# First products by block sums in tiles 3 to 6, with casts moved to GpSimd

## The chip, the cores and the metric

The kernel runs on one core of a Trainium2 chip. The metric is the device time of one execution in microseconds. The engines are TensorE (PE, with its weight loads shown apart as PEld), VectorE (DVE), ScalarE (ACT), GpSimd (POOL) and SyncE (SP, which only issues transfers here). GpSimd issues transfers too, between its own instructions.

## What is computed

Two stages follow each other: attention in a window of 32 positions, and a feed-forward block with the tanh form of GELU on its output.

```python
def _attn_ref(q, k, v):            # 8 batches, 8 heads, 576 positions, 64 wide
    scores = scale * np.matmul(q, k.transpose(0, 1, 3, 2))
    mask = np.abs(pos[:, None] - pos[None, :]) <= 32
    scores = np.where(mask, scores, -1000000000.0)
    attn = np.exp(scores - np.max(scores, axis=-1, keepdims=True))
    attn = attn / (np.sum(attn, axis=-1, keepdims=True) + 1e-09)
    return np.matmul(attn, v)

def _moe_ref(x, w_in, w_out):      # 4608 tokens, 512 wide, 2048 hidden
    h = x @ w_in
    g = 0.5 * h * (1.0 + np.tanh(c * (h + 0.044715 * h * h * h)))
    return g @ w_out
```

Everything comes and goes in float32; the products run in float16 with float32 sums.

## The kernel before

**Tiles.** The 4608 tokens are cut into nine tiles of 512, numbered t = 0 to 8. A batch holds 576 tokens, so batch b = t + 1 has its attention computed while tile t is in its second product, and its columns go into a ring `xT` of 1536 tokens.

**A tile's first stage** multiplies by `w_in`. The 2048 hidden columns are 16 blocks of 128, numbered n; block n stands at column `n // 2 + 8 * (n % 2)`. One block is four matmuls of 512 columns (`ffn_in`, L577), then one GELU on ScalarE (`gelu`, L585, or L657 in `in_mixed`) into `gT`. The first three matmuls of blocks 0 to 2 run ahead of the stage's last attention columns. After every fourth block `sums` (L694) forms four sums of GELU results on VectorE for the second stage.

**A tile's second stage** multiplies by `w_out` in steps i = 0 to 111, one matmul of 256 columns each (`ffn_out`, L751): seven products of 16 steps. This is the scheme of Strassen in Winograd's form, where four quarter matrices need seven products in place of eight, and sums of quarters are formed beforehand. The table `WINO` lists which sums are multiplied; `new` says that a product starts a bank instead of adding to it. After each product VectorE takes the result into `yo` (L762 to L789), which the next use of the same bank waits for. GpSimd issues the output stores (L713, L711) after product 5 and at the end.

**Attention in the second stage.** The dictionary `PLAN` hangs steps of attention onto the steps i: `s` scores and exponentials, `m` the mask on VectorE, `v` the weighted values and the denominators, `x` the multiplication into `xT` (L540). `@0` and `@1` name one of two pairs of PSUM banks, `S0` and `S1`; without one, `v` uses the banks `O` and `D`. Group -1 is the tail of the batch before.

**Queries and keys.** For b >= 4 these are loaded as float32 by SyncE (`load_qk`), cast to float16 on VectorE at the start of the tile's first stage (`turn_queries` L410, `turn_keys` L419, `turn_tails` L430), and turned by transposing transfers on SyncE's queue (L413, L421, L431). V is loaded and cast by a GpSimd transfer (L216, L220) at steps 4 and 7, after a small copy on GpSimd (`after`, L989) that waits for the key tail's transpose. `pair_v` (L225, L226) makes shifted copies of V on VectorE.

**Order.** Each engine runs its instructions in the order in which the program issues them; nothing rearranges them. A tile buffer that is used again waits for its last readers, and for a store that reads it until that store has landed.

**Tiles 7 and 8** do eight of their 16 blocks by seven products as well, in two groups of four blocks, A and B (`in_mixed`, L629). `in_w` forms four sums of quarters of `w_in` (L604), `in_x` four differences of quarters of `xT` (L614). The list `MIX` is the order of one such stage: a number is a plain block, `A0` or `B0` a product, `s0A` a copy of a bank into SBUF (L644), `cA00` an addition onto that copy (L649), `g` a GELU, and `t` and `u` the first and the last two of the four sums. A product that adds to a bank waits for the copy or the addition that reads it first. `WINO` and `MIX` share the same seven products:

```python
WINO = [("A11", "B11", True), ("S2", "T2", True), ("A12", "B21", False), ("S3", "T3", False),
        ("S1", "T1", True), ("A22", "T4", False), ("S4", "B22", False)]
```

**Buffers.** The pool `rawp` has two buffers each under the names `qr` and `kr`, 8 KB per partition, which take turns for raw queries, keys, V of batches 2 and 3, and in tiles 7 and 8 for `in_w`'s sums of A and the copies. The pool `yp` has two buffers under the name `yo`. They hold in turn two scratch tiles of batch 0, a score tile, the last two output row blocks of tile 0 (`yo` of `ffn_out_0`, kept in `later` and stored in tile 2), and the sums of group B.

Of the kernel before, what the change touches and what calls it, by code (L numbers as in the profile page):

```python
# [36 lines left out]
def cut(b):  # L37
# [5 lines left out]

PLAN = {7: "s0@0 s1@1 v-1", 16: "m0 m1 x-1", 33: "s2@0 v0@1 v1", 36: "m2", 44: "x0", 50: "x1",
        62: "s3@0 s4@1 v2", 66: "m3", 80: "x2", 84: "m4", 91: "v3", 112: "x3"}


# [11 lines left out]

MIX = ("3 g3 A0 s0A B0 s0B 12 g12 A2 B2 cA00 cB00 A1 s1A gA00 A4 B1 s1B gB00 B4 t0 u0 13 g13 A3 s3A B3 s3B 14 g14 "
       "cA11 cB11 A5 gA10 B5 gB10 gA11 gB11 A6 B6 cA01 cB01 15 gA01 gB01 t1 t2 g15 t3 u1 u2 u3").split()
UNITS = {"A": 1, "B": 2}

PLAN_1 = {12: "s0@0 s1@1 s2", 16: "m0 m1", 36: "m2", 56: "s-1@0 v0@1 v1", 62: "m-1 x0", 64: "x1",
# [4 lines left out]
          [(t4, 12 + i + j) for i in (0, 2) for t4 in (0, 3, 1, 2) for j in range(2)]  # L71


RING = 1536
LOW = -30000.0

# [2 lines left out]
def kernel(  # L79
# [26 lines left out]

    const = ctx.enter_context(tc.tile_pool(name="const", bufs=1))
    big = ctx.enter_context(tc.tile_pool(name="big", bufs=1))
    rawp = ctx.enter_context(tc.tile_pool(name="rawp", bufs=2))
    hp = ctx.enter_context(tc.tile_pool(name="hp", bufs=1))  # L110
    tailp = ctx.enter_context(tc.tile_pool(name="tailp", bufs=1))
    pep = ctx.enter_context(tc.tile_pool(name="pep", bufs=3))
# [24 lines left out]
    def load_early(b):  # L137


        qr = rawp.tile([128, H, 256], FP32, name="qr")  # L140
        kr = rawp.tile([128, H, 256], FP32, name="kr")
        raws[b] = [qr, kr, None]

        def qk(h0, queues=(nc.sync, nc.sync)):
            for src, dst, queue in zip((q, k), (qr, kr), queues):
                queue.dma_start(
                    dst[:, h0:h0 + 2, :],
                    src[b, h0:h0 + 2, 0:512, :].rearrange("h (p j) d -> p h (j d)", j=4))

        def vs(*cs):  # L150
            if len(raws[b]) < 4:
                raws[b].append(stage.tile([128, 4, H, 64], FP32, name="vr", tag="stage"))
                raws[b].append(tailp.tile([128, 4, 64], FP32, name="vt", tag="vt"))
            for c in cs:
                if c == 4:
                    for x in range(2):
                        nc.sync.dma_start(raws[b][4][64 * x:64 * x + 64, :, :],
                                          v[b, 4 * x:4 * x + 4, 512:S, :].rearrange("h p d -> p h d"))
                else:
                    nc.sync.dma_start(raws[b][3][:, c, :, :],  # L160
                                      v[b, :, 128 * c:128 * c + 128, :].rearrange("h p d -> p h d"))

        def tails(which="qk"):
            if raws[b][2] is None:
                raws[b][2] = tailp.tile([128, H, 64], FP32, name="tr", tag="tr")
            tr = raws[b][2]
            if b == 0:
                for i, src in enumerate((q, k)):
                    for x in range(2 if "qk"[i] in which else 0):
                        nc.sync.dma_start(tr[64 * x:64 * x + 64, 4 * i:4 * i + 4, :],  # L170
                                          src[b, 4 * x:4 * x + 4, 512:576, :].rearrange("h s d -> s h d"))
                return
            for h in (0, 4):
                for x, src in enumerate((q, k)):
                    nc.sync.dma_start(tr[64 * x:64 * x + 64, h:h + 4, :],
                                      src[b, h:h + 4, 512:576, :].rearrange("h s d -> s h d"))

        return qk, tails, vs

    def load_qk(b):  # L180


        if b == 3:
            qr = raws[3]
        else:
            qr = rawp.tile([128, H, 256], FP32, name="qr")
            load_q(b, qr)
        kr = rawp.tile([128, 4, H, 64], FP32, name="kr")
        if b > 3:
            qt = tailp.tile([16, H, 256], FP32, name="qt", tag="vt")  # L190
            kt = tailp.tile([64, H, 64], FP32, name="kt", tag="tr")
            raws[b] = (qr, kr, qt, kt)
        else:
            raws[b] = [qr, kr, tailp.tile([128, H, 64], FP32, name="tr", tag="tr"), None]
        for c in range(4):
            nc.sync.dma_start(kr[:, c, :, :],
                              k[b, :, 128 * c:128 * c + 128, :].rearrange("h p d -> p h d"))
        load_tails(b, nc.sync)
        if b == 3:
            load_vr(3)  # L200
# [199 lines left out]


    def load_vr(b):
        vr = vrs[b] = rawp.tile([128, 4, H, 64], FP32, name="qr")
        for c in range(4):
            nc.sync.dma_start(vr[:, c, :, :],
                              v[b, :, 128 * c:128 * c + 128, :].rearrange("h p d -> p h d"))

    def turn_queries(b, src, dst, p0, p1):
        for pr in range(NPAIR):
            nc.vector.tensor_copy(  # L410
                dst[:, pr, :, :, :].rearrange("p j h d -> p h j d"),
                src[:, 2 * pr:2 * pr + 2, :].rearrange("p h (j d) -> p h j d", j=4))
        nc.sync.dma_start_transpose(QTs[b].rearrange("d r j p -> d (r j) p")[:, :, p0:p1],  # L413
                                    dst.rearrange("p r j h d -> p (r j h d)"))

    def turn_keys(b):
        k16, kr = halfs[b][1], raws[b][1]
        for pr in range(NPAIR):
            nc.vector.tensor_copy(k16[:, pr, :, :, :], kr[:, :, 2 * pr:2 * pr + 2, :])  # L419
            if pr % 2:  # L420
                nc.sync.dma_start_transpose(  # L421
                    KTs[b % 2][:, pr - 1:pr + 1, :].rearrange("d r (c p) -> d (r c) p", c=4),
                    k16[:, pr - 1:pr + 1, :, :, :].rearrange("p r c h d -> p (r c h d)"))

    def turn_tails(b):
# [1 line left out]
        qt16 = hp.tile([16, NPAIR, 4, 2, 64], FP16, name="qt16", tag="qt16")  # L427
        kt16 = hp.tile([64, NPAIR, 2, 64], FP16, name="kt16", tag="t16")
        turn_queries(b, qt, qt16, 128, 144)
        nc.vector.tensor_copy(kt16.rearrange("p r h d -> p (r h d)"), kt.rearrange("p h d -> p (h d)"))  # L430
        nc.sync.dma_start_transpose(  # L431
            KLs[b % 2], kt16.rearrange("p r h d -> p (r h d)"))

# [157 lines left out]
    def in_w(eng, unit, *which):  # L591
# [1 line left out]
        i, j = UNITS[unit] // 2, 2 * (UNITS[unit] % 2)  # L593
        A11, A12, A21, A22 = (w_cols[:, d:d + 2, c + i, j:j + 2, :] for c in (0, 2) for d in (0, 2))
        if (unit, "s") not in mixed:
            halves = [(rawp if unit == "A" else yp).tile([128, 2, 2, 2, 128], FP16, name="wc" + unit + str(x),
                                                         tag=("qr", "kr")[x] if unit == "A" else "yo") for x in range(2)]
            mixed[unit, "s"] = [half[:, x] for half in halves for x in range(2)]
        S1, S2, S3, S4 = mixed[unit, "s"]
        mixed[unit, "w"] = dict(A11=A11, A12=A12, A22=A22, S1=S1, S2=S2, S3=S3, S4=S4)  # L600
        for x in which:
# [4 lines left out]
    def in_x(t):  # L606

        pos = t * 512 % RING
        B11, B12, B21, B22 = (xT[:, d:d + 2, pos + c:pos + c + 256] for d in (0, 2) for c in (0, 256))
        xc = hp.tile([128, 4, 2, 256], FP16, name="xc", tag="q16" if t % 2 else "k16")  # L610
        T1, T2, T3, T4 = (xc[:, x] for x in range(4))
        mixed["x"] = dict(B11=B11, B21=B21, B22=B22, T1=T1, T2=T2, T3=T3, T4=T4)
        for dst, a, b in ((T1, B12, B11), (T2, B22, T1), (T3, B22, B12), (T4, B21, T2)):
            nc.vector.tensor_tensor(dst, a, b, op=ALU.subtract)  # L614

    def in_product(unit, n):
        a, w, new = WINO[n]
        if n == 0:
            phs[unit, "a"] = psO.tile([128, 512], FP32, name="pu", tag="O") if unit == "A" else bank(1)
        elif n in (2, 4):  # L620
            which = "b" if n == 2 else "c"
            if unit == "A":
                phs[which] = psS.tile([128, 2, 512], FP32, name="pu2", tag="S1" if n == 2 else "S0")
            phs[unit, which] = phs[which][:, "AB".index(unit), :]
        ps = phs[unit, "b" if n == 2 else "c" if n in (4, 6) else "a"]
# [4 lines left out]
                                 start=(n in (0, 2, 4) and h == d == 0), stop=(h == d == 1), skip_group_check=True)  # L630

    def in_mixed(t):
        if "A" not in mixed:
            mixed["A"] = rawp.tile([128, 3, 512], FP32, name="sa", tag="qr")
            mixed["B"] = rawp.tile([128, 3, 512], FP32, name="sb", tag="kr")

        place = {"00": (0, "b"), "01": (1, "c"), "11": (2, "c")}
        for step in MIX:
            kind, rest = step[0], step[1:]
            if kind in UNITS:  # L640
                in_product(kind, int(rest))
            elif kind == "s":
                n, unit = int(rest[0]), rest[1]
                (nc.scalar.copy if n == 1 or rest == "3B" else nc.vector.tensor_copy)(  # L644
# [285 lines left out]
    for t in range(NT):  # L930
        b = t + 1
        att = b < B
        if t:
# [8 lines left out]
            elif att:  # L942
                if b > 3:
                    open_and_turn(b)
                turn_keys(b)
                if b > 3:
                    turn_tails(b)
            if t >= NT - 2:
                if t == NT - 2:
                    in_x(t)  # L950
                in_mixed(t)
            for fc in range(begun, NF if t < NT - 2 else 0):
                ffn_in(t, fc)
                if t == 1 and fc == 3:
                    turn_keys(2)
                    load_vr(2)
                    raws[2] = [None, None, raws[2][2], vrs[2], tailp.tile([64, H, 64], FP32, name="vt", tag="vt")]
                    nc.sync.dma_start(raws[2][4], v[2, :, 512:S, :].rearrange("h p d -> p h d"))
                    raws[3] = rawp.tile([128, H, 256], FP32, name="qr")
                    load_q(3, raws[3])  # L960
                    combine(4, nc.vector)
                if t == 1 and 6 <= fc < 10:
# [24 lines left out]
        for i in range(113 if t else 65):  # L987
# [67 lines left out]
                    spread(*group(g), *ods[g])  # L1055
            if t == NT - 2 and i == 84:
                in_x(t + 1)
            if t in (3, 4) and i == 52:
                in_w(nc.vector, "B", *((1, 2) if t == 3 else (3, 4)))
            if t == NT - 3 and i in (52, 86):  # L1060
                in_w(nc.vector, "A", *((1, 2) if i == 52 else (3, 4)))
            if t == 2 and i in (40, 44):
                store(0, *later[1 if i == 40 else 3])
            if t == 1 and i == 30:
                cast_vt(2)
                store(0, *later[0])
# [43 lines left out]
```

## Time and profile before

| | us |
|---|---|
| three runs | 297.32, 299.41, 296.19 |
| median | 297.32 |
| profiled execution | 296.65 |
| its span, first to last instruction | 294.6 |
| mean granted TensorE clock | 0.997 |
| start of the first stage of tiles 3, 4, 5, 6 and 7 | 115.67, 146.09, 176.57, 206.99, 237.40 |
| length of the first stage of tiles 3 to 6 | 13.8 |
| length of the first stage of tiles 7 and 8 | 13.3 |

A row of a timeline gives the start and the length in microseconds, the engine, the line, the operation, what it writes and reads, the shape, and how many like it were merged; in brackets stands how long the engine was idle before it and what ended that. L577 is line 577 of the listing. PE's matmuls overlap, so one that is shown with 379 ns follows the one before by less. "To landing" is the time from a transfer's issue to its end. A stage's row in the table by stage gives its limits, its length, and for each engine the busy time and the count.

### The profile page before, as it was taken

The numbers are of one execution on the slowest core, as the hardware profiler recorded it, in microseconds if no ns is written. First come the engines' busy times: TensorE is split into PE (matmuls) and PEld (weight loads), VectorE is DVE, ScalarE is ACT, GpSimd is POOL, SyncE is SP. The second block draws the span as 40 slices with busy tenths as digits, with TensorE's granted clock in tenths as the row PEclk, the third lists the DMA queues.
The fourth block names the chain that finished last, engine by engine and source line by source line (L and its number), as shares of the span: only waits on it lengthen the run. The fifth ranks groups of instructions, "written<-read, shape, count | busy, mean of one in ns | idle before, by whom it ended". The sixth has DMA issues, their size and how long they took to land.

```text
span 294.6 us, 7286 instructions
## 1 busy us (share of the span) xinstructions
PE 285.9 (97%) x2945; PEld 192.7 (65%) x2945; DVE 212.4 (72%) x467; ACT 196.5 (67%) x315; POOL 88.8 (30%) x143
## 2 busy tenths in 40 slices
PE   8889999999999999999999999999999999999993
PEld 3535545547765687568755885588558867887783
DVE  4755477998897667858796878686957877865762
ACT  5965877777677874787667776796669558706800
POOL 4445335004228713205250615050800050025000
PEclk9999999999999999999999999999999999999998
DMA  7999998999999998999999999899691040004013
GB/s 229 275 380 396 359 305 196 254 186 203 248 229 202 251 202 188 113 139 245 162 212 94 246 157 191 116 245 154 117 190 7 0 118 28 2 26 120 0 47 99
DMA packets 114392, 51.02 MB, mean 173 GB/s; under 512 B 98471, under 2 KB 110247, under 8 KB 114102
## 3 DMA queue, kind: packets, MB, share of 16 engines
q1 hardware_dynamic: 89460, 38.67, 62.4%
q0 software_dynamic: 23776, 10.83, 23.4%
q10 hardware_dynamic: 1122, 1.06, 1.1%
q8 instruction: 23, 0.38, 0.6%
q14 instruction: 11, 0.09, 0.1%
HBM read 36.70 MB, written 9.44 MB: 157 GB/s over the span
## 4 chain that ended last, share of the span: by engine, by line
PE 85%; DVE 5%; DMA 5%; issue 1%; SPq 1%; ACT 1%; POOL 0%; DVEq 0%
PE mm L751 32%; PE ph L577 17%; PE mm L577 16%; PE ps_s L468 4%; PE pu L629 3%; DMA kr<-in_k_dram 3%; PE mm L723 2%; DMA wst<-in_moe_w_in_dram 2%; PE py L723 2%; PE ps_d L495 2%; PE ps_o L505 2%; DVE t L684 2%; DVE s L694 1%; PE mm L629 1%; PE ps_od L495 1%; PE ps_od L505 1%
## 5 line engine op out<-in xcount | busy, mean ns | idle before, releaser
L577 PEld LDWEIGHTS <-w_in 128*128 128x128 f16 x512 | 57.4, 113 | 49.8 <-POOL w_in L250 1.5
L577 PE MATMUL ph<-xT,w_in 128*128 128x512 f16 x256 | 64.5, 379 | 0.6 <-POOL w_in L250 0.6
L577 PE MATMUL mm<-xT,w_in 128*128 128x512 f16 x256 | 64.1, 379 | 0.0
L585 ACT ACTIVATE gT<-mm 128x512 f16<-128x512 f32 x60 | 35.6, 598 | 33.3 <-PE mm L577 32.7
L713 POOL DMA_DIRECT2D out_dram<-y x55 | 32.8, 605 | 82.4 <-DVE y L780 75.3
L751 PEld LDWEIGHTS <-s 128*128 128x128 f16 x512 | 49.3, 98 | 7.1 <-DVE s L694 0.6
L751 PE MATMUL mm<-t,s 128*128 128x256 f16 x376 | 45.2, 273 | 0.2 <-DVE y L764 0.2
L694 DVE TENSOR_TENSOR s<-gT 128x512 f16<-128x512 f16 x64 | 27.5, 430 | 19.1 <-ACT gT L585 18.9
L751 PEld LDWEIGHTS <-gT 128*128 128x128 f16 x384 | 36.2, 98 | 6.4
L585 ACT ACTIVATE gT<-ph 128x512 f16<-128x512 f32 x58 | 32.4, 604 | 10.9 <-PE ph L577 10.9
L481 ACT ACTIVATE pe<-ps_s 128x960 f16<-128x960 f32 (+1 forms) x31 | 29.5, 975 | 13.2 <-PE ps_s L468 13.1
L751 PE MATMUL mm<-w_out,gT 128*128 128x256 f16 x256 | 32.6, 273 | 0.0
L104 ACT ACT_TABLE_LOAD x18 | 23.1, 1283 | 2.2 <-issue 1.9
L530 ACT ACTIVATE lt<-ps_d 128x480 f32<-128x480 f32 (+2 forms) x28 | 15.6, 556 | 10.4 <-PE ps_d L495 6.9
L531 ACT ACTIVATE lt<-lt 128x480 f32<-128x480 f32 (+3 forms) x36 | 21.1, 585 | 1.1
L490 DVE TENSOR_TENSOR pe<-pe,band 128x960 f16<-128x960 f16 x28 | 18.5, 680 | 2.0 <-ACT pe L481 1.9
L505 PEld LDWEIGHTS <-V 128*64 128x64 f16 x520 | 13.7, 111 | 5.5 <-DVE V L226 1.5
L751 PE MATMUL mm<-t,gT 128*128 128x256 f16 x128 | 16.1, 273 | 0.0
L694 DVE TENSOR_TENSOR s<-s,gT 128x512 f16<-128x512 f16 x32 | 14.0, 436 | 1.1
L216 POOL DMA_DIRECT2D V<-in_v_dram x16 | 14.3, 908 | 1.1 <-PE ps_s L468 0.4
L751 PE MATMUL mm<-w_out,s 128*128 128x256 f16 x120 | 14.6, 273 | 0.0
L540 DVE TENSOR_TENSOR xT<-ps_o,lt 128x480 f16<-128x480 f32 (+5 forms) x26 | 13.4, 535 | 1.6 <-PE ps_o L505 1.6
(149 smaller groups left out, 390.3 us busy)
## 6 DMA issues: line engine op xcount, KB each, us to landing
kr<-in_k_dram SPq DMA_DIRECT2D x31, 256.0 KB, 10.2
qr<-in_q_dram SPq DMA_DIRECT2D x6, 1024.0 KB, 5.9
wst<-in_moe_w_in_dram SPq DMA_DIRECT2D x8, 512.0 KB, 6.6
wst<-in_moe_w_out_dram SPq DMA_DIRECT2D x2, 1024.0 KB, 10.5
wst<-in_moe_w_out_dram SPq DMA_DIRECT2D x4, 512.0 KB, 7.4
qr<-in_v_dram SPq DMA_DIRECT2D x8, 256.0 KB, 6.5
V<-in_v_dram POOLq DMA_DIRECT2D x16, 128.0 KB, 8.5
qr<-in_q_dram SPq DMA_DIRECT2D x7, 256.0 KB, 7.3
```

Source lines behind the costliest of these rows:

```text
L104: nc.scalar.add_instruction(mybir.InstLoadActFuncSet(name=nc.get_next_instruction_name(), act_func_set_id=which, ins=[], outs=[]))
L216: nc.gpsimd.dma_start(V[:, c, :, :], v[b, :, 128 * c:128 * c + 128, :].rearrange("h p d -> p h d"))
L481: nc.scalar.activation(pe, ps[:, :, 0:w], AF.Exp, scale=SCALE)
L490: nc.vector.tensor_tensor(pe, pe, m.rearrange("k (o j) p -> k o j p", o=1).broadcast_to(list(pe.shape)), op=ALU.mult)
L505: nc.tensor.matmul(o[64 * h:64 * h + 64, cols].rearrange("d (j p) -> d j p", j=4)[:, :, p0 - q0:p1 - q0], Vs[b % 2][:, slot, 2 * pr + h, : ...
L530: nc.scalar.activation(lt[:, 0:n], d[:, 0:n], AF.Ln)
L531: nc.scalar.activation(lt[:, 0:n], lt[:, 0:n], AF.Exp, scale=-1.0)
L577: nc.tensor.matmul(ph, w_cols[:, dc, fc // 4, fc % 4, :], xT[:, dc, t * 512 % RING:t * 512 % RING + 512], start=(dc == 0), stop=(dc == 3))
L585: nc.scalar.activation(gTs[t][:, fc, :], phs[fc], AF.Gelu_apprx_tanh)
L694: nc.vector.tensor_tensor(dst, x, y, op=op)
L713: eng.dma_start(out_v[b, j, q0 + p:q0 + p + e, cols], yo[m:m + e, cols])
L751: nc.tensor.matmul(pys["apart"][:, 0:256] if apart else py[:, blk, :], lhsT, wino[w][:, f, :], start=(new and i % (8 if one else 16) == 0) ...
```

## The change

In tiles 3 to 6 the four blocks of group B (n = 8 to 11) are done by seven products, with a list `MIX_1` for the order, group A staying plain. The banks are those of group A in tiles 7 and 8. The key casts, the query-tail casts and the key-tail cast of batches 4 to 7 move from VectorE to GpSimd; the main query casts stay. `rawp` gets one buffer under each of four names, `q0`, `q1`, `k0` and `k1`. The sums of B's weights, formed in tiles 3 and 4 before, are formed in tile 2; the two stores of `yo` in tile 2 stand at steps 8 and 12 of the program instead of 40 and 44. `v1` moves from step 33 to step 36, and `pair_v` stands in `MIX_1`.

```diff
-PLAN = {7: "s0@0 s1@1 v-1", 16: "m0 m1 x-1", 33: "s2@0 v0@1 v1", 36: "m2", 44: "x0", 50: "x1",
+PLAN = {7: "s0@0 s1@1 v-1", 16: "m0 m1 x-1", 33: "s2@0 v0@1", 36: "m2 v1", 44: "x0", 50: "x1",
         62: "s3@0 s4@1 v2", 66: "m3", 80: "x2", 84: "m4", 91: "v3", 112: "x3"}
...
+MIX_1 = ("3 B0 g3 s0B 4 B2 cB00 B1 s1B g4 5 g5 6 g6 t0 u0 B3 s3B gB00 pair B4 7 g7 cB11 gB11 12 g12 t1 u1 B5 gB10 B6 cB01 gB01 13 g13 14 g14 t2 u2 15 g15 t3 u3").split()
...
+LONE = 3
...
-    rawp = ctx.enter_context(tc.tile_pool(name="rawp", bufs=2))
+    rawp = ctx.enter_context(tc.tile_pool(name="rawp", bufs=1))
...
     def turn_queries(b, src, dst, p0, p1):
         for pr in range(NPAIR):
-            nc.vector.tensor_copy(
+            (nc.gpsimd if p0 and b > LONE else nc.vector).tensor_copy(
...
     def turn_keys(b):
-            nc.vector.tensor_copy(k16[:, pr, :, :, :], kr[:, :, 2 * pr:2 * pr + 2, :])
+            (nc.gpsimd if b > LONE else nc.vector).tensor_copy(k16[:, pr, :, :, :], kr[:, :, 2 * pr:2 * pr + 2, :])
...
-        nc.vector.tensor_copy(kt16.rearrange("p r h d -> p (r h d)"), kt.rearrange("p h d -> p (h d)"))
+        (nc.gpsimd if b > LONE else nc.vector).tensor_copy(kt16.rearrange("p r h d -> p (r h d)"), kt.rearrange("p h d -> p (h d)"))
...
-        xc = hp.tile([128, 4, 2, 256], FP16, name="xc", tag="q16" if t % 2 else "k16")
+        xc = rawp.tile([128, 4, 2, 256], FP16, name="xc", tag="k1") if t < NT - 2 else \
+            hp.tile([128, 4, 2, 256], FP16, name="xc", tag="q16" if t % 2 else "k16")
...
-    def in_product(unit, n):
+    def in_product(unit, n, alone):
         a, w, new = WINO[n]
         if n == 0:
-            phs[unit, "a"] = psO.tile([128, 512], FP32, name="pu", tag="O") if unit == "A" else bank(1)
+            phs[unit, "a"] = psO.tile([128, 512], FP32, name="pu", tag="O") if unit == "A" or alone else bank(1)
         elif n in (2, 4):
             which = "b" if n == 2 else "c"
-            if unit == "A":
+            if unit == "A" or alone:
...
-        for step in MIX:
+        for step in MIX if t >= NT - 2 else MIX_1:
             kind, rest = step[0], step[1:]
-            if kind in UNITS:
-                in_product(kind, int(rest))
+            if step == "pair":
+                pair_v(t + 1, nc.vector.tensor_copy)
+            elif kind in UNITS:
+                in_product(kind, int(rest), t < NT - 2)
...
                 if b > 3:
                     open_and_turn(b)
+                if t >= LONE:
+                    in_x(t)
                 turn_keys(b)
                 if b > 3:
                     turn_tails(b)
...
-            for fc in range(begun, NF if t < NT - 2 else 0):
+            elif t >= LONE:
+                in_mixed(t)
+            for fc in range(begun, NF if t < LONE else 0):
...
-            if t in (3, 4) and i == 52:
-                in_w(nc.vector, "B", *((1, 2) if t == 3 else (3, 4)))
+            if t == LONE - 1 and i in (52, 86):
+                in_w(nc.vector, "B", *((1, 2) if i == 52 else (3, 4)))
...
-            if t == 2 and i in (40, 44):
-                store(0, *later[1 if i == 40 else 3])
+            if t == 2 and i in (8, 12):
+                store(0, *later[1 if i == 8 else 3])
```

Left out above are the new tags in the calls that allocate from `rawp`.

More of the change, by code (lines that the diff above doesn't have):

```diff
@@ L137, in load_early @@
     def load_early(b):
-        qr = rawp.tile([128, H, 256], FP32, name="qr")
-        kr = rawp.tile([128, H, 256], FP32, name="kr")
+        qr = rawp.tile([128, H, 256], FP32, name="qr", tag=f"q{b}")
+        kr = rawp.tile([128, H, 256], FP32, name="kr", tag=f"k{b}")
         raws[b] = [qr, kr, None]
@@ L185, in load_qk @@
         else:
-            qr = rawp.tile([128, H, 256], FP32, name="qr")
+            qr = rawp.tile([128, H, 256], FP32, name="qr", tag="q0")
             load_q(b, qr)
-        kr = rawp.tile([128, 4, H, 64], FP32, name="kr")
+        kr = rawp.tile([128, 4, H, 64], FP32, name="kr", tag="k1" if b == 3 else "k0")
         if b > 3:
@@ L402, in load_vr @@
     def load_vr(b):
-        vr = vrs[b] = rawp.tile([128, 4, H, 64], FP32, name="qr")
+        vr = vrs[b] = rawp.tile([128, 4, H, 64], FP32, name="vr", tag="q1")
         for c in range(4):
@@ L595, in in_w @@
         if (unit, "s") not in mixed:
-            halves = [(rawp if unit == "A" else yp).tile([128, 2, 2, 2, 128], FP16, name="wc" + unit + str(x),
-                                                         tag=("qr", "kr")[x] if unit == "A" else "yo") for x in range(2)]
-            mixed[unit, "s"] = [half[:, x] for half in halves for x in range(2)]
+            if unit == "A":
+                wc = rawp.tile([128, 4, 2, 2, 128], FP16, name="wcA", tag="q0")
+                mixed[unit, "s"] = [wc[:, x] for x in range(4)]
+            else:
+                halves = [yp.tile([128, 2, 2, 2, 128], FP16, name="wcB" + str(x), tag="yo") for x in range(2)]
+                mixed[unit, "s"] = [half[:, x] for half in halves for x in range(2)]
         S1, S2, S3, S4 = mixed[unit, "s"]
@@ L632, in in_mixed @@
     def in_mixed(t):
-        if "A" not in mixed:
-            mixed["A"] = rawp.tile([128, 3, 512], FP32, name="sa", tag="qr")
-            mixed["B"] = rawp.tile([128, 3, 512], FP32, name="sb", tag="kr")
+        if "B" not in mixed:
+            mixed["B"] = rawp.tile([128, 3, 512], FP32, name="sb", tag="q1")
+        if t == NT - 2:
+            mixed["A"] = rawp.tile([128, 3, 512], FP32, name="sa", tag="k0")
         place = {"00": (0, "b"), "01": (1, "c"), "11": (2, "c")}
-        for step in MIX:
+        for step in MIX if t >= NT - 2 else MIX_1:
             kind, rest = step[0], step[1:]
-            if kind in UNITS:
-                in_product(kind, int(rest))
+            if step == "pair":
+                pair_v(t + 1, nc.vector.tensor_copy)
+            elif kind in UNITS:
+                in_product(kind, int(rest), t < NT - 2)
             elif kind == "s":
@@ L958 @@
                     nc.sync.dma_start(raws[2][4], v[2, :, 512:S, :].rearrange("h p d -> p h d"))
-                    raws[3] = rawp.tile([128, H, 256], FP32, name="qr")
+                    raws[3] = rawp.tile([128, H, 256], FP32, name="qr", tag="q0")
                     load_q(3, raws[3])
```

## The prediction

> **What bounds the kernel now.** I read the page's first lines, then the table by stage, then the chain, then the timelines of single engines around the places that the change touches.
>
> ```profile
> span 294.6 us, 7286 instructions
> PE 285.9 (97%) x2945; PEld 192.7 (65%) x2945; DVE 212.4 (72%) x467; ACT 196.5 (67%) x315; POOL 88.8 (30%) x143
> ```
>
> TensorE is busy for 97% of the span, so a change gains only by giving it less to do and loses by whatever makes it stand still. By stage (columns: stretch and length, then busy time of PE, PEld, DVE, ACT, POOL with counts, clock, DMA share, GB/s) it looks like this; the first three rows are tile 2's second products, tile 6's first products and tile 7's first products:
>
> ```profile
> 99.07:115.67 16.60, 16.60 (x268) 13.74 (x266) 11.26 (x20) 12.91 (x18) 5.56 (x9) 1.00 1.31 220
> ...
> 206.99:220.80 13.81, 13.81 (x66) 7.25 (x65) 10.83 (x29) 8.63 (x15) 5.74 (x9) 1.00 0.94 160
> ...
> 237.40:250.72 13.32, 13.32 (x90) 9.39 (x89) 8.99 (x19) 8.67 (x17) 4.10 (x8) 1.00 0.28 79
> ```
>
> TensorE fills each stage to the last tenth, VectorE uses 10.8 of the 13.8 us of a first stage, and the DMA engines are full until tile 6 starts. A wait of any engine for a DMA in tiles 1 to 5 is therefore a long one.
>
> **Part 1, the products.** Four blocks are 16 matmuls of 512 columns; the chain spends 0.86 us on four, 0.216 us each, so 3.46 us. Seven products are 28 matmuls of 256 columns; the chain spends 0.44 us on four (0.109 us each), so 3.06 us. That is 0.40 us less per tile and 1.6 us in four tiles. The two rows above give less, 13.81 - 13.32 = 0.49 us for two groups, 0.25 us each and 1.0 us in all, since TensorE waits at two places of tile 7. I take 1.6 here and count waits apart.
>
> **Part 2, the block sums of the weights.** `in_w` for group B (four additions at L604, 0.68 us each) leaves the second stages of tiles 3 and 4 and is put into that of tile 2, at steps 52 and 86. The additions by themselves cost nothing: tiles 3 and 4 hold two of them each, tile 5 none, and from the start of one first stage to the next they take 30.42, 30.48 and 30.42 us (115.67, 146.09, 176.57, 206.99). VectorE's idle time hides them. But their target is the two `yo` buffers, which in tile 2 still hold the last output rows of tile 0, and these leave by a store. The diff moves the stores from steps 40 and 44 to 8 and 12. GpSimd's order is not changed by this: it issues them right behind the V loads in both versions and does not wait for step 40 today.
>
> ```profile
> 97.97 0.19 POOL L989 COPY after<-KL 128x1 f16<-128x1 f16 x1 [1.08 <-ACT KL L358]
> 98.53 3.58 POOL L216 DMA_DIRECT2D V<-in_v_dram  x4 [0.36 <-PE mm L577]
> 102.35 0.69 POOL L220 DMA_DIRECT2D V<-in_v_dram  x1 [0.24 <-issue]
> 103.03 1.13 POOL L713 DMA_DIRECT2D out_dram<-yo  x2
> ```
>
> ```profile
> DMA to landing us min/median/max: 13.8/13.9/13.9
> ```
>
> Those are GpSimd's timeline in tile 2 and the landing time of the two stores. They go out at 103.03 and 103.60, behind five V loads on the same queue (9.1 to 13.7 us to landing), and land near 116.9 and 117.4. VectorE reaches step 52 far earlier:
>
> ```profile
> 107.49 0.65 DVE L540 TENSOR_TENSOR xT<-ps_o,lt 128x480 f16<-128x480 f32 x1
> 109.80 0.69 DVE L771 TENSOR_TENSOR y<-mm,y 128x512 f32<-128x512 f32 x1 [1.66 <-PE mm L751]
> 110.41 0.65 DVE L490 TENSOR_TENSOR pe<-pe,band 128x960 f16<-128x960 f16 x1
> ```
>
> ```profile
> 111.34 1.36 PE L751 MATMUL mm<-t,gT 128*128 128x256 f16 x11
> ```
>
> The first row is step 50's spread, so the first addition wants to start at 108.1 and waits until 116.9. Queued behind it on VectorE are L771 (product 3's result), the mask of group 3, L774 and the next spread. TensorE runs on until product 5, step 80 (last row, 111.4), which adds into the bank that L771 has to read first. VectorE then needs two additions (1.3 us) and L771 (0.69): 116.9 + 2.0 = 118.9. TensorE stands for 118.9 - 111.4 = 7.5 us. Bounds: nothing, if the stores land before 108.1, and about 9 us if they land as late as 118.5. I take 7.5, since queue and order are those of this profile. Step 86's two additions come after 117.4 and find the other buffer free.
>
> A stand of that length also costs clock. At the span's end TensorE stops at 290.0, and the granted clock is 0.50 from 292.9 on, 2.9 us later. At its start the warming matmuls (L288) take 0.63 us from 1.3 us on and 0.38 us from about 6.2 us on, so the fast clock comes after 4.9 us of work. Half the speed for 4.9 us loses 2.4 us; I take 2.2, as a little of it lies under the wait for the spread of step 80. The bounds are 0 and 2.4. Tile 2 thus costs 9.7 us.
>
> The Trainium skill ("TensorE: Matmul & The Clock Gate", Part 1) puts the fall and the return at one window of about 3.4 us each; an estimate from that page alone would be 1.7 us lost instead of 2.4. Either way the rule speaks against a long stand of TensorE.
>
> **Part 3, what VectorE gains and loses in tiles 3 to 6.** It loses the four key casts, four query-tail casts and the key-tail cast (9 instructions, 0.34 to 0.38 us apart, 3.3 us). It gains `in_x` (four subtractions of 0.42, 1.5 us with their overlap), the copy `s0B` (0.69) and three additions L649 (0.69 each, 0.6 apart). That is 3.9 us, a net of 0.6, and the 3 us of idle time in the stage would hide it. ScalarE gets two copies more (0.58 each) and has 5 us idle. Laid out on tile 4 (stage start 146.1), `in_x` ends at 149.8 behind the query casts; product 1 may start when `s0B` is done at 150.5, and TensorE gets there at 151.1. So these cost nothing alone.
>
> **Part 4, the nine casts on GpSimd.** They queue behind the output stores; in tile 4 these end at 151.7, in the others 4.3 to 5.8 us into the stage. From there VectorE's sums run against them. How that goes can be seen in tile 1, where GpSimd casts V:
>
> ```profile
> 89.22 0.43 DVE L694 TENSOR_TENSOR s<-gT 128x512 f16<-128x512 f16 x1 [1.42 <-ACT gT L585]
> 89.68 0.42 DVE L694 TENSOR_TENSOR s<-s,gT 128x512 f16<-128x512 f16 x1
> 90.03 0.83 DVE L694 TENSOR_TENSOR s<-gT 128x512 f16<-128x512 f16 x1
> 90.78 0.82 DVE L694 TENSOR_TENSOR s<-gT,s 128x512 f16<-128x512 f16 x1
> ```
>
> ```profile
> 89.83 1.50 POOL L993 CAST V<-qr 128x512 f16<-128x512 f32 x2 [0.92 <-DMA qr<-in_v_dram]
> ```
>
> A sum takes 0.42 us alone and 0.82 beside a cast, a cast 0.61 alone and 0.75 beside a sum: they take turns. In tile 4 the four sums t0 and u0 start at 151.9 and then end near 155.0 instead of 153.3; the pair copies (0.69 and 0.55) lose 0.35 us each and end near 156.9 instead of 154.6; `cB11` behind them ends at 157.5. TensorE wants B6 at 156.3, and B6 adds into the bank that `cB11` reads: 1.2 us of standing. The casts of keys themselves are not late for the scores: two casts end near 153.3, the first key transpose goes out at 152.07 today and SyncE is full with the query transpose until 152.0, so it moves by about 1 us, while the scores that need it move by 0.8. Late next is the copy of group 01, and with it the last block's GELU, whose bank the denominators at step 7 need: 0.6 us in tiles 4 and 6, where the stores end late, 0.1 in tiles 3 and 5. Together 1.2 + 0.3 = 1.5 us per tile, 6.0 in four. Below, it costs nothing, if the casts fall into VectorE's idle time; above, if all nine casts hold up a VectorE instruction for their full 0.61 us against the 3 us of slack, 2.5 us per tile, 10 in all. I take 6.0, because the rows of tile 1 show the same kinds of instruction beside each other.
>
> The Trainium skill ("SBUF — State Buffer", Who interferes with whom) says that a VectorE instruction with two SBUF inputs and a GpSimd instruction that reads SBUF lock each other out completely. By it a sum would wait for a whole cast, 0.61 + 0.42 = 1.03 us per turn, and four sums would take 4.1 us instead of 3.1, so some 1 us more per tile. The rows show 0.82 and decide.
>
> **Part 5, the rest.** Single raw buffers: SyncE issues the next loads only behind the last key transpose, which needs all casts done, so the one buffer is always free by then; 0 us, at worst the 1 us per tile by which GpSimd's last cast moves that transpose. The key and tail casts that read these loads come some 4 us later than today's, so loads later by 1 us are still early. v1 moved by three steps: 0.3 us later in an order that TensorE runs anyway, 0.
>
> **Sum.** The profiled execution took 296.65 us (span 294.6 and 2.05 around it), 0.67 below the median of the runs, 297.32. 296.65 + 9.7 - 1.6 + 6.0 = 310.8 us.
>
> **Rivals.** (a) The stores land before VectorE gets to step 52, so only Part 4 costs: 296.65 - 1.6 + 6.0 = 301.1, slower still. For it: the fastest V load takes 9.1 us. Against: the two rows of 13.9. (b) Not slower: the stores are early and the casts find idle time, only the products count: 296.65 - 1.6 = 295.1, within 1%; a saving of 2.3 us would be faster by 1% than the median. It decides if `cB11` ends before B6 in each tile and no addition waits in tile 2. For it: VectorE's 3 us of idle time in each first stage. Against: both parts need an accident that this profile does not show. (c) Part 2 as forecast, no loss in Part 4, but the first key transpose lands after the scores by 1 us per tile: 296.65 + 9.7 - 1.6 + 4.0 = 308.8; for it, that transpose follows the query one through a full DMA.
>
> **How the numbers follow.** Forecast 0.62, (a) 0.12, (b) 0.18, (c) 0.08. The forecast's own range is 302.5 (Part 4 and the clock at nothing) to 316 (Part 4 at 10, landing 1 us later). Down to 300 it takes in (a); (b) is left out. A difference under about 1%, 3 us, can't be told from none here. Faster by over 1% is a third of (b), 0.06; within 1% the other two thirds, 0.12; slower 0.82.
>
> **What would show it.** In tile 2, a VectorE wait of about 8.8 us for the `out_dram` store ahead of wcB L604, a TensorE gap of about 7.5 us ahead of product 5, and a granted clock of 0.5 behind it. In tiles 3 to 6, first stages of 14.5 us or more against 13.8, with B6 waiting for `cB11` and sums of 0.8 us beside casts on POOL. The prediction is wrong if L604 in tile 2 does not wait, or if the first stages of tiles 3 to 6 last 13.4 us.

## The result, and the profile after

The changed kernel takes 314.84 us in the median of six runs (311.0 to 316.24), the kernel before 297.37. The ratio is 1.0555 with a 95% interval of 1.0483 to 1.0627: slower by 5.6%. Ratios, here and below, leave out runs more than 1.5% above the fastest of the same kernel; here that is the one of 316.24 us. The profiled execution took 312.99 us, its span is 310.8 us. The engine lines of its page:

```profile
span 310.8 us, 7443 instructions
PE 288.8 (93%) x2993; PEld 197.5 (64%) x2993; DVE 226.0 (73%) x463; ACT 197.7 (64%) x323; POOL 113.9 (37%) x179
```

TensorE fell from 97% to 93% of a longer span: it stands idle for 22.0 us (310.8 - 288.8), against 8.7 before. The table by stage shows where. The rows are tile 2's second stage and the first stages of tiles 3 to 6, with the columns as before:

```profile
100.06:125.67 25.61, 18.41 (x267) 14.38 (x266) 13.71 (x24) 12.91 (x18) 5.68 (x8) 0.87 0.81 138
125.67:140.45 14.78, 13.74 (x78) 8.29 (x77) 13.14 (x26) 8.62 (x18) 10.51 (x17) 1.00 0.94 150
157.28:172.28 15.00, 13.74 (x79) 8.28 (x77) 13.04 (x26) 8.69 (x18) 12.24 (x19) 1.00 0.82 148
189.17:203.93 14.76, 13.74 (x79) 8.29 (x77) 13.13 (x26) 8.62 (x18) 10.48 (x17) 1.00 0.94 149
220.75:236.73 15.98, 13.74 (x78) 8.30 (x77) 13.97 (x26) 8.69 (x18) 11.48 (x18) 1.00 0.73 141
```

Measured in the same way, from first matmul to first matmul, the kernel before takes 16.60 us for the first of these and 13.81 or 13.82 for the others. So tile 2 costs 9.0 us (25.61 - 16.60) and the four first stages 5.3 (60.52 - 55.25). The second stages of tiles 3 to 6 add 0.9 in all (16.82 to 16.89 us each, against 16.60 to 16.67). That stage of tile 2 began at 100.06 us, against 98.91 before: 1.15 us. Ahead of it only the raw buffers and their names differ, and in the runs below with the same code there it began anywhere from 98.9 to 103.0 us, so the 1.15 us can't be put down to the change. From tile 7 on the two kernels take the same, within 0.1 us. 9.0 + 5.3 + 0.9 + 1.15 - 0.1 = 16.2 us, the whole difference of the spans.

VectorE's timeline in tile 2, then TensorE's:

```profile
108.87 0.65 DVE L542 TENSOR_TENSOR xT<-ps_o,lt 128x480 f16<-128x480 f32 x1
118.01 0.69 DVE L609 TENSOR_TENSOR wcB<-w_in 128x512 f16<-128x512 f16 x1 [8.49 <-DMA out_dram<-yo]
118.74 0.69 DVE L609 TENSOR_TENSOR wcB<-wcB,w_in 128x512 f16<-128x512 f16 x1
119.34 0.68 DVE L780 TENSOR_TENSOR y<-mm,y 128x512 f32<-128x512 f32 x1
```

```profile
120.08 2.50 PE L760 MATMUL mm<-t,gT 128*128 128x256 f16 x11 [7.20 <-DVE y L780]
```

The additions of `in_w` (now L609) wait 8.49 us for the store of `yo`. L780, the result of product 3 (before: L771), stands behind them, and TensorE waits 7.20 us for it ahead of product 5. Its eleven matmuls then take 2.50 us against 1.36 before: the clock has fallen. The granted clock, third from the end, is 0.50 from 116.4 to 123.2 us:

```profile
116.40:123.20 6.80, 3.12 (x23) 1.89 (x24) 5.16 (x9) 0.03 (x1) 0.00 (x0) 0.50 0.05 11
```

In the first stages of tiles 3 to 6 TensorE stands ahead of product 6 (B6), for the addition `cB11` (now L658). These are tiles 4 and 6:

```profile
168.78 0.60 PE L635 MATMUL pu<-xT,wcB 128*128 128x256 f16 x4 [0.94 <-DVE sb L658]
...
233.52 0.60 PE L635 MATMUL pu<-xT,wcB 128*128 128x256 f16 x4 [2.22 <-DVE sb L658]
```

### The profile page after: what moved, and what is told of

It is laid out like the page before. It is cut to its first block, busy times and chain, and to the rows that moved or that the text cites. A ratio compares the mean times of both kernels' runs of the same rounds, so it can differ in the third digit from the quotient of the medians.

```text
span 310.8 us, 7443 instructions
## 1 busy us (share of the span) xinstructions
PE 288.8 (93%) x2993; PEld 197.5 (64%) x2993; DVE 226.0 (73%) x463; ACT 197.7 (64%) x323; POOL 113.9 (37%) x179
## 4 chain that ended last, share of the span: by engine, by line
PE 69%; DVE 13%; DMA 8%; SPq 3%; issue 2%; POOL 1%; ACT 1%; ACTq 0%; DVEq 0%; POOLq 0%
PE mm L760 29%; PE ph L579 12%; PE mm L579 9%; DVE s L703 5%; PE pu L635 5%; DMA out_dram<-yo 4%; PE ps_s L470 3%; DMA wst<-in_moe_w_in_dram 3%; PE mm L732 2%; PE py L732 2%; PE ps_d L497 2%; DVE sb L658 2%; SPq L273 2%; DVE t L693 1%; PE ps_o L507 1%
## 5 line engine op out<-in xcount | busy, mean ns | idle before, releaser
L579 PEld LDWEIGHTS <-w_in 128*128 128x128 f16 x448 | 50.1, 113 | 41.3 <-POOL w_in L252 2.8
L722 POOL DMA_DIRECT2D out_dram<-y x55 | 30.7, 567 | 93.5 <-DVE y L789 83.1
L579 PE MATMUL ph<-xT,w_in 128*128 128x512 f16 x240 | 60.5, 379 | 1.7 <-POOL w_in L252 1.6
L579 PE MATMUL mm<-xT,w_in 128*128 128x512 f16 x208 | 53.7, 379 | 0.0
L703 DVE TENSOR_TENSOR s<-gT 128x512 f16<-128x512 f16 x64 | 32.2, 503 | 8.9 <-ACT gT L587 5.8
L483 ACT ACTIVATE pe<-ps_s 128x960 f16<-128x960 f32 (+1 forms) x31 | 29.5, 975 | 13.8 <-PE ps_s L470 13.7
L587 ACT ACTIVATE gT<-mm 128x512 f16<-128x512 f32 x28 | 16.5, 599 | 25.6 <-PE mm L579 25.4
L587 ACT ACTIVATE gT<-ph 128x512 f16<-128x512 f32 x38 | 20.9, 605 | 7.0 <-PE ph L579 7.0
L662 ACT ACTIVATE gT<-sb 128x512 f16<-128x512 f32 x18 | 11.5, 637 | 9.9 <-DVE sb L658 9.9
L507 PEld LDWEIGHTS <-V 128*64 128x64 f16 x520 | 14.1, 112 | 5.1 <-DVE V L228 1.3
L703 DVE TENSOR_TENSOR s<-s,gT 128x512 f16<-128x512 f16 x32 | 15.4, 480 | 1.1
L703 DVE TENSOR_TENSOR s<-gT,s 128x512 f16<-128x512 f16 x32 | 15.4, 480 | 0.0
L666 ACT ACTIVATE gT<-ph 128x512 f16<-128x512 f32 x22 | 13.2, 600 | 3.3 <-PE ph L579 3.2
```

The costliest lines, as they stand in the source:

```text
L483: nc.scalar.activation(pe, ps[:, :, 0:w], AF.Exp, scale=SCALE)
L507: nc.tensor.matmul(o[64 * h:64 * h + 64, cols].rearrange("d (j p) -> d j p", j=4)[:, :, p0 - q0:p1 - q0], Vs[b % 2][:, slot, 2 * pr + h, : ...
L579: nc.tensor.matmul(ph, w_cols[:, dc, fc // 4, fc % 4, :], xT[:, dc, t * 512 % RING:t * 512 % RING + 512], start=(dc == 0), stop=(dc == 3))
L587: nc.scalar.activation(gTs[t][:, fc, :], phs[fc], AF.Gelu_apprx_tanh)
L703: nc.vector.tensor_tensor(dst, x, y, op=op)
L722: eng.dma_start(out_v[b, j, q0 + p:q0 + p + e, cols], yo[m:m + e, cols])
```

## The experiments

All are small edits of one of the two kernels. "Early stores" is the base of most of them.

**Early stores.** The stores go ahead of the V loads on GpSimd's queue.

```diff
-            if t == 2 and i in (8, 12):
-                store(0, *later[1 if i == 8 else 3])
+            if t == 2 and i in (0, 1):
+                store(0, *later[1 if i == 0 else 3])
```

> The changed kernel, with the two stores of tile 0's rows issued at steps 0 and 1 of tile 2, so ahead of the V loads on GpSimd's queue. Theory A (the additions wait for the store's landing): the stores go out near 98 us and land within 8 us, the wait of 8.5 us ahead of wcB and the gap of 7.2 us on TensorE vanish, the granted clock stays at 1.00, tile 2's second stage takes 16.6 to 17.0 us instead of 25.6, and the kernel gains about 9 us (near 304 us). Rival B (the four additions themselves are too much for VectorE in tile 2): the second stage stays above 20 us, since they stand where they stood. Tiles 3 to 6 are the same in both, 31.6 to 32.8 us from one first stage to the next.

304.4 us, ratio 1.0178 to the kernel before (1.0120 to 1.0237). The stage of tile 2, VectorE's timeline in it and the stores' landing:

```profile
98.91:115.73 16.82, 16.82 (x267) 13.78 (x266) 13.40 (x24) 12.84 (x18) 4.37 (x6) 1.00 1.24 215
```

```profile
107.84 0.64 DVE L542 TENSOR_TENSOR xT<-ps_o,lt 128x480 f16<-128x480 f32 x1
108.41 0.68 DVE L609 TENSOR_TENSOR wcB<-w_in 128x512 f16<-128x512 f16 x1
```

```profile
DMA to landing us min/median/max: 10.3/10.4/10.5
```

The same additions stand at the same place and now cost nothing: the stage takes 16.82 us, 8.79 less. Theory A holds, rival B falls. The landing was expected within 8 us and took 10.4; the stores left at 96.8 and landed near 107.2, barely 1 us ahead of the additions. The first stages of tiles 4 to 6 kept their length (14.99, 14.75 and 15.98 us); tile 3's grew from 14.78 to 15.23 us, where B6 waits 1.46 us.

**Stores at their old steps.** Does the place in the program matter, or only the place in GpSimd's queue?

```diff
-            if t == 2 and i in (8, 12):
-                store(0, *later[1 if i == 8 else 3])
+            if t == 2 and i in (40, 44):
+                store(0, *later[1 if i == 40 else 3])
```

> The changed kernel, with the two stores of tile 0's rows back at steps 40 and 44 of tile 2. Theory A: GpSimd has them behind the same V loads and reaches them at the same time, so they are issued within 1 us of the V loads' end, land 13 to 14 us later, and TensorE stands 7 us as before: 311 to 315 us, no difference. Rival: the place in the program matters, and the stores leave later, with a longer wait by the 2 to 3 us between the steps.

One run of 312.65 us. GpSimd issues the stores at 103.92 and they land after 13.7 us:

```profile
103.24 0.73 POOL L222 DMA_DIRECT2D V<-in_v_dram  x1
103.92 1.18 POOL L722 DMA_DIRECT2D out_dram<-yo  x2
```

VectorE waits 7.9 us, TensorE 6.64, and the stage takes 25.38 us. The result is as expected: this edit moves the stores by 32 steps of the program and past nothing on GpSimd. What counts is their place among GpSimd's instructions.

**Matmuls during the stand.** This separates the clock's part from the wait's.

```diff
+            if t == 2 and i == 80:
+                spin(28, 512, psS.tile([128, 2, 512], FP32, name="warm", tag="S0")[:, 0, :])
```

> The changed kernel, with 28 matmuls of 512 columns into an unused bank ahead of step 80 of tile 2, about 6 us of work that fills most of the 7.2 us for which TensorE stands there. Theory A2 (part of the loss in tile 2 is the clock that falls during that stand): the granted clock stays at 1.00, the stand shrinks to about 1 us, and from the end of the result L780 to the first matmul of tile 3 it takes about 4.3 us instead of 5.8; the kernel is about 1.5 us faster than the changed one. Rival (the clock plays no part, the 5.8 us are waits for VectorE): still 5.8 us.

The stage of tile 2 in this kernel, then TensorE's timeline:

```profile
100.63:125.26 24.63, 23.20 (x295) 16.50 (x294) 13.50 (x24) 12.91 (x18) 5.14 (x8) 1.00 0.91 159
```

```profile
113.29 6.21 PE L290 MATMUL warm<-KT 128*128 128x512 f16 x28
120.88 1.36 PE L760 MATMUL mm<-t,gT 128*128 128x256 f16 x11 [1.38 <-DVE y L780]
```

The clock stayed at 1.00 and product 5 took 1.36 us again. From L780's end to tile 3's first matmul it took 4.44 us (120.82 to 125.26), against 5.65 in the changed kernel (120.02 to 125.67). So the clock's part is 1.2 us, not the 1.5 expected. The whole time of this one run, 313.67 us, did not gain: the stage began 0.6 us later, the wait ended at 118.80 us against 118.01, and tile 6 lost 1.5 us to the clock in another place (below).

**No casts on GpSimd.** Early stores, and zero fills in place of the nine casts, shown for the keys; the query and key tails likewise.

```diff
-            (nc.gpsimd if b > LONE else nc.vector).tensor_copy(k16[:, pr, :, :, :], kr[:, :, 2 * pr:2 * pr + 2, :])
+            if b > LONE:
+                nc.gpsimd.memset(k16[:, pr, :, :, :], 0.0)
+            else:
+                nc.vector.tensor_copy(k16[:, pr, :, :, :], kr[:, :, 2 * pr:2 * pr + 2, :])
```

> As the one before, but the nine casts of each of tiles 3 to 6 on GpSimd are left out, and a fill with zeros, which reads nothing, stands in the place of each, so that the scores of batches 4 to 7 are of zeros. Theory C (sums on VectorE and casts on GpSimd hold each other up): the sums beside them take 0.42 us again instead of 0.7 to 0.8, cB11 ends ahead of B6, the first stages of tiles 3 to 6 take 13.4 to 13.6 us instead of 14.6 to 15.8; the kernel is about 4.5 us faster than the one before. Rival D (VectorE has too much to do of its own, with the differences, copies and additions): VectorE keeps its order and its work, so the first stages stay at 14.4 us or more.

One run of 297.72 us, 6.7 us less than the median of early stores, where about 4.5 were expected. The first stages of tiles 3 to 6, then VectorE and GpSimd in tile 6:

```profile
117.66:131.08 13.42, 13.42 (x78) 8.31 (x77) 11.54 (x27) 8.82 (x18) 9.81 (x17) 1.00 1.12 170
147.91:161.32 13.41, 13.41 (x78) 8.29 (x77) 11.45 (x26) 8.76 (x18) 10.40 (x19) 1.00 1.01 160
178.21:191.63 13.42, 13.42 (x78) 8.31 (x77) 11.45 (x26) 8.76 (x18) 8.96 (x17) 1.00 1.02 165
208.46:221.96 13.50, 13.50 (x79) 8.30 (x77) 11.49 (x26) 8.68 (x18) 10.34 (x18) 1.00 0.94 165
```

```profile
214.46 0.41 DVE L709 TENSOR_TENSOR s<-gT 128x512 f16<-128x512 f16 x1
214.91 0.43 DVE L709 TENSOR_TENSOR s<-s,gT 128x512 f16<-128x512 f16 x1
...
213.86 1.94 POOL L425 MEMSET k<- 128x512 f16 x4
```

TensorE is busy for the whole of each stage. VectorE kept its own work and its order, so rival D falls: what delayed the sums were GpSimd instructions that read while VectorE wanted to. The Trainium skill ("SBUF — State Buffer", Who interferes with whom) says that a two-input instruction on VectorE contends with a GpSimd instruction that reads, not with one that only writes; the 0.41 us of a sum beside fills agrees. Only the sums were freed: in tile 4 the two copies of V took 1.04 and 0.86 us beside fills, much as beside casts in the changed kernel (1.00 and 0.87), and B6 did not wait all the same. And here the bare gain of the products shows: 13.81 - 13.42 = 0.39 us per tile.

**Casts back on VectorE.** Early stores, and all casts where they were before.

```diff
-            (nc.gpsimd if b > LONE else nc.vector).tensor_copy(k16[:, pr, :, :, :], kr[:, :, 2 * pr:2 * pr + 2, :])
+            nc.vector.tensor_copy(k16[:, pr, :, :, :], kr[:, :, 2 * pr:2 * pr + 2, :])
```

> As the first, but all casts stay on VectorE, where they stand behind the differences of xT. Theory C: no sum takes over 0.5 us, but nine casts of 0.35 us stand ahead of the copy s0B, which product 1 waits for: TensorE waits about 2.5 us there, and the first stages take 15 to 16 us. So moving the casts was needed for this order, and the kernel comes out near 303 to 306 us. Rival D': VectorE gets through, since it had 3 us of idle time: first stages at 13.4 us, 296 us.

312.37 us in the median of four runs (307.91 to 313.09), ratio 1.0368 (1.0252 to 1.0484), above the 303 to 306 expected. VectorE, then TensorE in tile 4 of the profiled run, the fastest:

```profile
152.95 1.53 DVE L421 CAST k<-kr 128x512 f16<-128x512 f32 x4
154.40 1.41 DVE L412 CAST qt<-qt 16x512 f16<-16x512 f32 x4
155.73 0.41 DVE L432 CAST kt<-kt 64x512 f16<-64x512 f32 x1
156.07 0.67 DVE L653 COPY sb<-pu 128x512 f32<-128x512 f32 x1
...
156.79 1.01 PE L635 MATMUL pu<-xc,wcB 128*128 128x256 f16 x4 [2.21 <-DVE sb L653]
```

The copy `s0B` comes behind all nine casts, and TensorE waits 2.1 to 2.2 us for it ahead of product 1 in each of the four tiles: first stages of 15.65, 17.43, 15.78 and 15.65 us. So moving the casts was no mistake as such; in this order of VectorE's work they cost more when left. The excess of the 17.43 us is the clock, as the last section tells. The other three runs have a lower mean clock too, 0.969 to 0.986 against 0.991, but no trace of them shows where.

**Casts alone.** The kernel before, with the nine casts on GpSimd and nothing else.

```diff
-            nc.vector.tensor_copy(k16[:, pr, :, :, :], kr[:, :, 2 * pr:2 * pr + 2, :])
+            (nc.gpsimd if b > 3 else nc.vector).tensor_copy(k16[:, pr, :, :, :], kr[:, :, 2 * pr:2 * pr + 2, :])
```

> The kernel before, with the nine casts of batches 4 to 7 on GpSimd and nothing else changed. Theory C (the casts cost only because a product in the first stage waits for an addition that stands behind sums held up by them): sums beside the casts take 0.7 to 0.8 us here too, but no block of the plain order waits for VectorE, so the stages stay at 13.8 and 16.6 us and the kernel within 1 us of the kernel before. Rival E (casts on GpSimd cost by themselves, by late key transposes or late sums): 0.5 to 1.5 us per tile, 300 to 303 us, with a TensorE gap ahead of the scores L468 or of product 1 of the second stage.

298.68 us, ratio 1.0026 (0.9992 to 1.0059), no difference that can be told. Every first stage takes 13.81 or 13.82 us, every second one 16.60 to 16.67, and the profiled span is 294.6 us, that of the kernel before. Yet the sums are held up here as well; the mean of the first kind of sum over the kernel is 525 ns against 430 before:

```profile
L694 DVE TENSOR_TENSOR s<-gT 128x512 f16<-128x512 f16 x64 | 33.6, 525 | 19.1 <-ACT gT L585 18.9
```

The contention costs only where TensorE waits for something that stands behind a sum. Rival E falls: in this order the casts cost nothing by themselves, by late key transposes either.

**Copies of V later.** Early stores, `pair` behind `cB01` instead of ahead of `cB11`, v1 back at step 33.

```diff
-... g6 t0 u0 B3 s3B gB00 pair B4 7 g7 cB11 gB11 12 g12 t1 u1 B5 gB10 B6 cB01 gB01 13 ...
+... g6 t0 u0 B3 s3B gB00 B4 7 g7 cB11 gB11 12 g12 t1 u1 B5 gB10 B6 cB01 gB01 pair 13 ...
-33: "s2@0 v0@1", 36: "m2 v1"
+33: "s2@0 v0@1 v1", 36: "m2"
```

> As the first, but the shifted copies of V stand behind the addition cB01 instead of ahead of cB11, and v1 is back at step 33. Theory C: the sums beside casts still take 0.7 to 0.8 us, but what TensorE waits for is no longer behind the two copies (1.9 us beside casts): B6 does not wait, first stages of tiles 3 to 6 take 13.4 to 13.9 us, and the second stages lose the 0.2 us that moving v1 cost; the kernel takes 295.5 to 298 us, within 1% of the kernel before. Rival D: VectorE is short of time whatever the order: the wait only moves to the end of the stage, first stages stay at 14.4 us or more, 302 us.

299.2 us, ratio 1.0008 (0.9966 to 1.0051): no difference from the kernel before that can be told, though the median lies above the 295.5 to 298 us expected. First stages take 13.71, 14.00, 13.41 and 14.46 us, two of them above the 13.9 expected; tile 6 is the longest:

```profile
210.55:225.01 14.46, 13.74 (x79) 8.30 (x77) 13.16 (x24) 8.70 (x18) 11.01 (x18) 1.00 0.95 153
```

In tile 6 B6 still waits 0.31 us for `cB11`, and the second stages of tiles 4 and 6 begin 0.4 us late for a GELU. The four together take 55.58 us, 5.4 less than with early stores (60.95), but 1.8 more than without casts (53.75): 0.5 us per tile is still lost, a little more than the products gain. Second stages are back at 16.60 to 16.67 us, so v1's move cost 0.22 us per tile; tile 2 shows it alone (16.82 against 16.60), since no copy of V moved there.

**Tail casts on ScalarE.** The version before, with the four query-tail casts as steps `z0` to `z3` on ScalarE.

```diff
-... B2 cB00 B1 s1B g4 5 g5 6 g6 t0 u0 B3 s3B gB00 B4 7 g7 cB11 ...
+... B2 cB00 B1 z0 z1 s1B g4 5 g5 6 g6 z2 t0 u0 B3 s3B gB00 B4 7 g7 z3 cB11 ...
+            if kind == "z":
+                nc.scalar.copy(qt16[:, pr, :, :, :].rearrange("p j h d -> p h j d"),
+                               qt[:, 2 * pr:2 * pr + 2, :].rearrange("p h (j d) -> p h j d", j=4))
```

> As the version with late copies of V and v1 back at step 33, and the four query-tail casts are on ScalarE, which idles 1.4 us ahead of the copy s1B; five casts per tile are left on GpSimd. Theory C: four sums instead of eight are held up, tiles 4 and 6, where the output stores end late, lose their remaining waits (0.3 to 0.4 us ahead of product 6 and of the second stage), first stages come to 13.4 to 13.5 us in all four, and the kernel is 1 to 1.5 us faster than the kernel before (ratio 0.995 to 0.997). Rival: ScalarE is then short of time, and a GELU comes late for a bank: first stages of 13.8 us or more, ratio 1.000 to 1.005.

296.36 us, ratio 0.9957 (0.9922 to 0.9992): faster than the kernel before by 0.4%, with an interval that ends just short of 1, and so the fastest version here. All four first stages take 13.53 us or less; tile 6 as an example:

```profile
205.94:219.46 13.52, 13.52 (x78) 8.30 (x76) 12.24 (x24) 10.42 (x22) 8.01 (x14) 1.00 0.98 158
```

13.81 - 13.53 = 0.28 us per tile, 1.1 in four, against 1.56 without any cast. The 0.11 us per tile between the two lies ahead of the second stage's first matmul; the rows put it behind a GELU, but the trace lists no wait there.

## Why the prediction was right, point by point

The direction, the place of both losses and the size hold: 310.8 us was forecast (300 to 316), 312.99 is the profiled execution and 314.84 the median. That the total came this near owes something to luck: tile 2 was put 0.9 us too high without v1 (9.7 against 8.8), the first stages 0.9 too low, v1's 1.1 us was not counted, and the late start of 1.15 us is nobody's forecast.

- **Part 1.** 0.40 us per tile forecast, 0.39 measured where nothing waits.
- **Part 2, the wait.** VectorE 8.8 us forecast, 8.49 measured; TensorE 7.5 against 7.20. Early stores show its cause, the old steps show that only the queue's order matters.
- **Part 2, the clock.** 2.2 us forecast, 1.2 measured. The failing term is the length of the slow clock: I gave it 4.9 us of work from the start of the execution. It fell at 116.4 and came back at 123.2, so only 3.1 us of it lay behind the resumed work. The deduction for the spread was right in kind: at full clock, in the run with matmuls in the stand, the spread (L542) ends at 122.56 us and the matmuls L507 that follow it start at 122.61, 0.2 us late. Tile 2 as a whole: 9.7 forecast, 9.0 measured, 0.2 of it v1.
- **Part 3.** Held: in the run without casts VectorE carries all its other new work and TensorE does not stand.
- **Part 4.** 1.5 us per tile forecast, 1.7 measured (60.52 - 53.75 = 6.8 us against the run without casts, in four tiles). B6 waits for `cB11`, 0.94 to 1.01 us idle in tiles 3 to 5 and 2.22 in tile 6; TensorE's busy time is longer as well, 13.74 us against 13.42 without casts. The second wait came too, but smaller: 0.32 us in tile 4 ahead of the second stage's first matmul, not at step 7 as I had it, and none that the trace lists in tile 6. The key transposes were not late: the casts alone cost nothing, and the second stages of the changed kernel are longer by no more than v1's 0.22 us.
- **Part 5.** v1 was put at 0 and cost 0.22 us in each of five second stages, 1.1 us in all. Split from v0, it costs one more change between kinds of matmul. Tile 2's rows agree: with early stores a full matmul follows the first L507 after 0.33 us, with v1 back the next L497 follows after 0.23; and the three full matmuls between take 0.43 us until the next L497, where three in a row take 0.33. The single buffers were not tried alone; the fastest version has them.

VectorE and GpSimd in tile 6 show why it lost most:

```profile
226.75 1.98 DVE L703 TENSOR_TENSOR s<-gT 128x512 f16<-128x512 f16 x1
...
229.40 0.82 DVE L703 TENSOR_TENSOR s<-gT 128x512 f16<-128x512 f16 x1
230.15 0.82 DVE L703 TENSOR_TENSOR s<-gT,s 128x512 f16<-128x512 f16 x1
230.99 1.00 DVE L227 COPY V<-V 64x2048 f16<-64x2048 f16 x1
232.00 0.87 DVE L228 COPY V<-V 64x1536 f16<-64x1536 f16 x1
232.80 0.67 DVE L658 TENSOR_TENSOR sb<-pu,sb 128x512 f32<-128x512 f32 x1
```

```profile
226.16 2.28 POOL L421 CAST k<-kr 128x512 f16<-128x512 f32 x4
```

The forecast had sum and cast take turns. The last two sums do, but the first took 1.98 us and ended only behind three more casts; the copies of V and `cB11` stand behind it.

## What to carry to other kernels

When an edit gives new data to an old buffer, look up when the last reader of that buffer ends, stores included, and in which queue that store stands; a step's place in the program says nothing about a queue that runs ahead of it. Work moved to an idle engine can slow the engine that it was meant to free, and then the price is not the contention but what stands behind it: with the same casts on GpSimd the plain order lost nothing, one order of seven products lost 1.7 us per tile, and another that keeps the waited-for additions ahead of the copies of V lost 0.5. A gain of 0.4 us in 13.8 is worth only what such an order leaves of it: nothing in that order, and 0.3 with the four query-tail casts on ScalarE.

## What the runs showed that I had not expected

**A stand of 2.2 us can cost the clock.** In the version with casts back on VectorE, TensorE stood 2.07 to 2.21 us in four tiles. In tile 4 alone the clock then fell; the rows are the stand, what followed, and the return:

```profile
154.60:156.70 2.10, 0.00 (x0) 0.00 (x0) 2.10 (x6) 0.00 (x0) 0.31 (x1) 1.00 1.27 232
156.80:160.10 3.30, 3.30 (x10) 1.47 (x10) 3.19 (x7) 1.63 (x3) 0.00 (x0) 0.50 0.76 107
160.20:163.00 2.80, 2.80 (x19) 1.78 (x18) 0.76 (x2) 2.07 (x4) 0.00 (x0) 1.00 1.10 158
```

That stage took 17.43 us where the others took 15.65 to 15.78. The same happened in tile 6 of the kernel with matmuls in the stand (17.50 us, clock 0.90), after 2.23 us; in the changed kernel's profile and with early stores the same 2.22 us did not touch it. So it depends on more than the length of the stand. The Trainium skill ("TensorE: Matmul & The Clock Gate", Part 1) puts the fall at an idle window of about 3.4 us that runs freely; a fall after 2.2 us is sooner than that rule says, and what else decides is open here. The runs of the changed kernel spread in the same sense, 311.0 and 312.99 us at a mean clock of 0.989, 314.42 to 316.24 at 0.972 to 0.980; in which stage the slower ones lost it no trace shows.

**One sum can wait through several casts.** Besides the 1.98 us above, a sum of 2.53 us stands in tile 6 of the fastest version, through three key casts and the key-tail cast, which follow each other without a pause, and costs nothing there:

```profile
211.93 2.53 DVE L713 TENSOR_TENSOR s<-gT 128x512 f16<-128x512 f16 x1
```
